# One load queue, 4 MB chunks and a hand-fixed order in an attention decode with a gated mixer

## The chip, the cores and the metric

The kernel runs on one core of one Trainium2 chip. The metric is the device time of one execution in microseconds (us), the median of several executions; lower is better. A profiled execution gives a "span", which is the same execution seen by the hardware profiler and about 2 us shorter than the device time.

## The reference, cut to what matters

One token attends to a cache of 65536 keys: 8 K/V heads, 16 query heads, head size 256. Beside it a small mixer makes a row `b`, and a gate mixes the two.

```python
x = A_x                                           # [1, 1, 448], all inputs bf16
g = sigmoid((x * gate_w).sum(-1))
q = (x @ wq)                                      # 16 heads of 256
s = einsum("bhqd,bhkd->bhqk", q, k) * 256**-0.5   # k_cache [1, 8, 65536, 256]
a = softmax(s) @ v                                # v_cache [1, 8, 65536, 256]
a = a.reshape(1, 1, 4096) @ wo
h = layernorm(x)                                  # the mixer: 448 x 1792 elements of gelu
u = gelu(einsum("bsd,sf->bdf", h, w1) + b1)       # w1 [1, 1792]
b = (einsum("bdf,fs->bds", u, w2) + b2)           # w2 [1792, 1]
out = g * a + (1 - g) * b
```

K and V are 537 MB of the 544 MB that have to be read. So this is first of all a matter of how fast one core can take data in.

## The kernel before

It walks through K and V in chunks of 2048 keys (1 MB of K, 1 MB of V, each a row of 8 KB for each of 128 partitions). K goes through the SyncE queue into 4 buffers, V through the ScalarE queue into 5. Each chunk of K is transposed on TensorE (32 transposes of 128x128 bf16), evicted by VectorE (copied out of PSUM, where matmuls leave their results) in four pieces of 128x1024, multiplied by q to give scores, put through `exp`, transposed in 32x32 blocks by VectorE, and multiplied by V. The order of instructions is chosen by an automatic scheduler; the code gives only the data flow. The mixer's 14 blocks stand in one piece behind the first head.

```python
CH = 2048
NJ = CH // 128
NKN = 4
NKT = 2
NVBUF = 5
# ...
    const = ctx.enter_context(tc.tile_pool(name="const", bufs=1))
# ...
    kn_tiles = [knpool.tile([128, NJ, DH], BF16, name=f"kn{i}") for i in range(NKN)]
    v_tiles = [vpool.tile([128, NJ, DH], BF16, name=f"vt{i}") for i in range(NVBUF)]
# ...
            k_src = A_k_cache[0, g, t0:t0 + CH, :].rearrange("(p j) d -> p j d", j=NJ)
            nc.sync.dma_start(out=kn[:, :, :], in_=k_src)
            v_src = A_v_cache[0, g, t0:t0 + CH, :].rearrange("(p j) d -> p j d", j=NJ)
            nc.scalar.dma_start(out=vt[:, :, :], in_=v_src)

            bank_i = 0
            for c in range(2):
                for j0 in range(0, NJ, 8):
                    tp = tps[bank_i % 2]
                    for jj in range(8):
                        j = j0 + jj
                        nc.tensor.transpose(tp[:, jj * 128:(jj + 1) * 128],
                                            kn[:, j, c * 128:(c + 1) * 128], ident[:, :])
                    nc.vector.tensor_copy(out=kT[:, c, j0:j0 + 8, :],
                                          in_=tp[:, :].rearrange("p (j n) -> p j n", j=8))
                    bank_i += 1
            # ... scores of this chunk: 8 matmuls of 512 columns
            if pending is not None:
                pv_matmuls(pv, *pending)          # P times V of the chunk before
            # ... exp on ScalarE
            nc.vector.transpose(out=pT[:, :], in_=p_sb[:, :])
            pending = (pT, vt, (ck == 0), (ck == n_chunks - 1))
        pv_matmuls(pv, *pending)
        if g == 0:
            mixer_mlp()                           # 14 blocks in one piece
        # ... normalise, turn and multiply by wo: the head's epilogue
```

The softmax here doesn't subtract the row's maximum and nothing guards it: scores larger than these inputs give would overflow.

## Time and profile before

| | before |
|---|---|
| median of 3 runs | 1354.73 us (1353.54 to 1356.97) |
| profiled span | 1353.1 us |
| data moved, rate on the plateau | 546.4 MB, 420 GB/s |
| PE, DVE, ACT busy | 73%, 65%, 15% |
| an 8 KB packet of K or V | 312 ns median |

In profiles PE stands for TensorE, PEld for its weight loads, DVE for VectorE, ACT for ScalarE, POOL for GpSimd and SP for SyncE; a q behind a name, as in SPq, is that engine issuing DMAs. From the page of the kernel before: busy time of each engine, two of the lines that cut the span into 40 equal slices (busy tenths of the DMA engines, and what they moved), then the load queues, the instruction fetch and the data read.

```profile
span 1353.1 us, 33043 instructions
PE 990.1 (73%) x14602; PEld 658.7 (49%) x14602; DVE 876.8 (65%) x1665; ACT 196.7 (15%) x554; POOL 8.2 (1%) x21
...
DMA  9999997899999999999999999999999999999994
GB/s 279 396 418 420 419 420 324 350 420 420 419 420 420 420 419 419 420 419 420 419 415 411 420 420 413 418 418 416 420 414 413 418 419 416 420 401 419 419 420 181
...
q1 hardware_dynamic: 37250, 272.12, 49.2%
q10 hardware_dynamic: 36864, 268.45, 48.3%
...
q8 instruction: 114, 1.87, 0.6%
...
HBM read 544.22 MB, written 0.00 MB: 402 GB/s over the span
```

No compute engine is near its limit. The DMA engines are, in nearly every slice. A slice is 33.8 us long. Where it shows 420 the kernel can only become faster if the stream itself does; where it shows less, something else held the stream up. This gives a ledger. For each slice the lost time is its length times (1 − its rate ÷ the plateau's rate); what remains of the span is the stream. The plateau is read off the slices, and one GB/s more or less there moves about 3 us between the stream and the other terms.

| us | stream at its plateau | lost in slices 0–1 (start) | 2–7 (mixer) | 8–37 (middle) | 38–39 (end) |
|---|---|---|---|---|---|
| before, 420 GB/s | 1300.9 | 13.3 | 13.6 | 6.0 | 19.2 |

The dip in slices 6 and 7 is the mixer. The table by stretches of the kernel before shows it: stretch, its length, busy time (and instructions) of PE, weight load, DVE, ACT and POOL, then the granted PE clock, the DMA share and GB/s. The last two lines are the end, where the data stops.

```profile
220.00:230.00 10.00, 9.66 (x81) 5.38 (x79) 5.90 (x11) 1.80 (x4) 0.00 (x0) 0.67 0.53 209
230.00:240.00 10.00, 10.00 (x71) 4.69 (x73) 7.76 (x18) 2.79 (x6) 0.00 (x0) 0.67 0.73 285
...
1335.00:1340.00 5.00, 3.43 (x59) 2.37 (x57) 3.46 (x8) 0.80 (x4) 0.00 (x0) 1.00 0.20 84
1340.00:1345.00 5.00, 2.88 (x55) 1.40 (x52) 3.08 (x7) 0.69 (x2) 0.00 (x0) 1.00 0.01 3
```

In these 20 us PE is full while the clock is down to 0.67, and the stream is at half to two thirds of its rate: there the mixer, not DMA, bounds the kernel. At the end 15 us of serial work remain after the last data. The PE lines of the timeline (start, duration, what it is, in brackets the idle time before it and what ended it) show its two ends:

```profile
1335.66 0.61 PE L295 MATMUL tps_128<-ident,kn_112 128*128 128x128 bf16 x8 [0.34 <-DVE kT_114 L300]
1337.92 0.56 PE L295 MATMUL tps_127<-ident,kn_113 128*128 128x128 bf16 x7 [0.90 <-DMA kn_113<-in_A_k_cache_dram]
...
1344.46 0.61 PE L260 MATMUL pv_ps_135<-vt_116,pT_124 128*2 128x256 bf16 x16 [1.66 <-DVE pv_sb L336]
```

The second line is the last time that PE waits for data. The first one also gives a cost: eight bf16 transposes in 0.61 us.

### The profile page before, as it was taken

Reading aid. Unit: us, or ns where it says so; the run is one execution under the profiler, and the core shown is the slowest. Engines: PE = TensorE matmul, PEld = TensorE weight load, DVE = VectorE, ACT = ScalarE, POOL = GpSimd, SP = SyncE. Lnnn points to the kernel's source line nnn. Section 1 sums busy time; section 2 is a strip of 40 time slices with the busy share of each in tenths; the row PEclk is TensorE's granted clock in tenths of the full one; section 3 lists DMA queues with packets and bytes.
Section 4 is the critical chain, followed back from the end, with each engine's and each line's share of the span. In section 5 each row is a group of like instructions: output and inputs, shape, how many; then the busy total and the mean of one; then the engine's idle time right before and its main releaser. Section 6 shows DMA issues by size and latency. Waiting matters only on the chain. (4 is left out here: it accounts for less than half of the span.)

```text
span 1353.1 us, 33043 instructions
## 1 busy us (share of the span) xinstructions
PE 990.1 (73%) x14602; PEld 658.7 (49%) x14602; DVE 876.8 (65%) x1665; ACT 196.7 (15%) x554; POOL 8.2 (1%) x21
## 2 busy tenths in 40 slices
PE   2887889867687776776677666767768767777775
PEld 2555555545454454544445444544445444544453
DVE  1567677866666666666666666666666666666665
ACT  0111122111111111111111111111111111111111
POOL 2000000000000000000000000000000000000000
PEclk9989897998999889899998999999999999989988
DMA  9999997899999999999999999999999999999994
GB/s 279 396 418 420 419 420 324 350 420 420 419 420 420 420 419 419 420 419 420 419 415 411 420 420 413 418 418 416 420 414 413 418 419 416 420 401 419 419 420 181
DMA packets 75281, 546.37 MB, mean 404 GB/s; under 512 B 8657, under 2 KB 8674, under 8 KB 9490
## 3 DMA queue, kind: packets, MB, share of 16 engines
q1 hardware_dynamic: 37250, 272.12, 49.2%
q10 hardware_dynamic: 36864, 268.45, 48.3%
q0 software_dynamic: 1024, 3.69, 0.7%
q8 instruction: 114, 1.87, 0.6%
q14 instruction: 29, 0.24, 0.0%
HBM read 544.22 MB, written 0.00 MB: 402 GB/s over the span
## 5 line engine op out<-in xcount | busy, mean ns | idle before, releaser
L300 DVE COPY kT_115<-tps_127 128x1024 bf16<-128x1024 bf16 x256 | 175.1, 684 | 137.2 <-PE tps_127 L295 136.7
L300 DVE COPY kT_114<-tps_127 128x1024 bf16<-128x1024 bf16 x256 | 174.9, 683 | 126.0 <-PE tps_127 L295 125.1
L300 DVE COPY kT_115<-tps_128 128x1024 bf16<-128x1024 bf16 x256 | 173.2, 677 | 85.1 <-PE tps_128 L295 81.9
L300 DVE COPY kT_114<-tps_128 128x1024 bf16<-128x1024 bf16 x256 | 173.5, 678 | 84.5 <-PE tps_128 L295 82.0
L295 PEld LDWEIGHTS <-kn_111 128*128 128x128 bf16 x2048 | 128.9, 103 | 150.2 <-DMA kn_111<-in_A_k_cache_dram 94.3
L295 PEld LDWEIGHTS <-kn_112 128*128 128x128 bf16 x2048 | 128.2, 103 | 140.9 <-DMA kn_112<-in_A_k_cache_dram 80.0
L295 PEld LDWEIGHTS <-kn_113 128*128 128x128 bf16 x2048 | 126.7, 102 | 135.5 <-DMA kn_113<-in_A_k_cache_dram 77.8
L295 PEld LDWEIGHTS <-kn_110 128*128 128x128 bf16 x2048 | 126.4, 102 | 126.6 <-DMA kn_110<-in_A_k_cache_dram 74.0
L319 ACT ACTIVATE p_sb_122<-sc_ps_133 128x512 bf16<-128x512 f32 x128 | 76.4, 597 | 545.1 <-issue 348.6
L319 ACT ACTIVATE p_sb_121<-sc_ps_132 128x512 bf16<-128x512 f32 x128 | 76.4, 597 | 515.3 <-issue 346.8
L295 PE MATMUL tps_127<-ident,kn_111 128*128 128x128 bf16 x1024 | 86.4, 230 | 78.2 <-DMA kn_111<-in_A_k_cache_dram 68.6
L295 PE MATMUL tps_127<-ident,kn_112 128*128 128x128 bf16 x1024 | 88.0, 230 | 65.0 <-DMA kn_112<-in_A_k_cache_dram 50.7
L295 PE MATMUL tps_127<-ident,kn_113 128*128 128x128 bf16 x1024 | 87.1, 230 | 66.2 <-DMA kn_113<-in_A_k_cache_dram 57.9
L295 PE MATMUL tps_127<-ident,kn_110 128*128 128x128 bf16 x1024 | 84.7, 228 | 58.2 <-DMA kn_110<-in_A_k_cache_dram 47.3
L308 PE MATMUL sc_ps_133<-kT_115,qT_sb 128*2 128x512 bf16 x1024 | 117.4, 401 | 0.4 <-DVE kT_115 L300 0.4
L308 PE MATMUL sc_ps_132<-kT_114,qT_sb 128*2 128x512 bf16 x1024 | 112.5, 396 | 0.5 <-DVE kT_114 L300 0.3
L295 PE MATMUL tps_128<-ident,kn_111 128*128 128x128 bf16 x1024 | 88.8, 231 | 15.7 <-DVE kT_115 L300 15.6
L295 PE MATMUL tps_128<-ident,kn_112 128*128 128x128 bf16 x1024 | 87.7, 230 | 15.2 <-DVE kT_114 L300 14.9
L295 PE MATMUL tps_128<-ident,kn_110 128*128 128x128 bf16 x1024 | 85.2, 227 | 16.9 <-DVE kT_114 L300 16.9
L295 PE MATMUL tps_128<-ident,kn_113 128*128 128x128 bf16 x1024 | 85.7, 228 | 14.5 <-DVE kT_115 L300 14.5
L326 DVE STREAM_TRANSPOSE pT_124<-p_sb_122 128x512 bf16<-128x512 bf16 x128 | 90.0, 703 | 0.0
L326 DVE STREAM_TRANSPOSE pT_123<-p_sb_121 128x512 bf16<-128x512 bf16 x128 | 89.9, 702 | 0.0
(101 smaller groups left out, 613.9 us busy)
## 6 DMA issues: line engine op xcount, KB each, us to landing
kn_110<-in_A_k_cache_dram SPq DMA_DIRECT2D x64, 1024.0 KB, 16.3
kn_111<-in_A_k_cache_dram SPq DMA_DIRECT2D x64, 1024.0 KB, 16.5
kn_112<-in_A_k_cache_dram SPq DMA_DIRECT2D x64, 1024.0 KB, 16.5
kn_113<-in_A_k_cache_dram SPq DMA_DIRECT2D x64, 1024.0 KB, 16.5
vt_116<-in_A_v_cache_dram ACTq DMA_DIRECT2D x52, 1024.0 KB, 15.3
vt_117<-in_A_v_cache_dram ACTq DMA_DIRECT2D x51, 1024.0 KB, 15.3
vt_118<-in_A_v_cache_dram ACTq DMA_DIRECT2D x51, 1024.0 KB, 15.2
vt_119<-in_A_v_cache_dram ACTq DMA_DIRECT2D x51, 1024.0 KB, 15.3
```

What stands on the lines that cost most here:

```text
L295: nc.tensor.transpose(tp[:, jj * 128:(jj + 1) * 128], kn[:, j, c * 128:(c + 1) * 128], ident[:, :],)
L300: nc.vector.tensor_copy(out=kT[:, c, j0:j0 + 8, :], in_=tp[:, :].rearrange("p (j n) -> p j n", j=8))
L308: nc.tensor.matmul(ps[32 * a:32 * a + 2, :], lhsT=qT_sb[:, c, 2 * g:2 * g + 2], rhs=rhs, start=(c == 0), stop=(c == 1), tile_position=(0, ...
L319: nc.scalar.activation(out=p_sb[:, :], in_=ps[:, :], func=ACT.Exp, scale=inv_sqrt_dh, accum_out=den[:, 0:1],)
L326: nc.vector.transpose(out=pT[:, :], in_=p_sb[:, :])
```

## The change

It is a rewrite with five intents: load everything through one queue in 4 MB chunks, of which 5 lie in a ring in turn (K, V, K, V, ...); transpose K as 32-bit pairs of bf16, which halves the number of transposes; fix the order of all instructions by hand; spread the mixer over the first 30 steps instead of one block; and shorten the epilogue. A step is still 2048 keys, a quarter of a chunk, and there are 256 of them. The product with V lags four steps behind. The core of the new code:

```diff
+    ctx.enter_context(tc.manual_schedule())
+    ring = [ringp.tile([128, NB * DH], BF16, name=f"ring{i}") for i in range(RING)]   # 5 x 32 KB a partition
+    LAST_V = [2 * SB, SB, SB // 2 + 2, SB // 2 - 2]
+    def load(item):                      # even items are K, odd ones V
+        ...
+        parts = [NB]                     # one DMA of 4 MB, rows of 32 KB
+        if i == total - 1:
+            parts = LAST_V if is_v else LAST_K
+        j = 0
+        for n in parts:
+            nc.sync.dma_start(out=dst[:, j * DH:(j + n) * DH], in_=src[:, j * DH:(j + n) * DH])
+            j += n
-                        nc.tensor.transpose(tp[...], kn[:, j, c * 128:(c + 1) * 128], ident[:, :])   # bf16, x32
+        kn = ring[2 * (n // STEPS) % RING][:].bitcast(FP32).rearrange("p (j k) -> p j k", k=128)
+        for jj in range(8):                                                           # fp32, x16
+            nc.tensor.transpose(tp[:, 128 * jj:128 * jj + 128], kn[:, j0 + jj, :], ident[:])
+        nc.vector.tensor_copy(out=kT[n % 2][...], in_=tp[:].bitcast(BF16))            # 128x2048, x2
+    def mixer_close(b):
+        nc.vector.scalar_tensor_tensor(out=gel[:], in0=t_b[:], scalar=1.0, in1=u_b[:], ...)
+        nc.tensor.matmul(y_ps, lhsT=w2T[:, b:b + 1], rhs=gel[:], start=(b == 0), stop=(b == NF - 1))
+    def mixer(n):
+        b, ph = divmod(n - 2, 2)
+        if ph == 0:
+            if 0 < b <= NF:
+                mixer_close(b - 1)
+            if b == NF:
+                mixer_end()
+            if 0 <= b < NF:
+                mixer_open(b)
+        elif 0 <= b < NF:
+            mixer_mid(b)
+    for n in range(n_steps + LAG):
+        transposes(n, 0)
+        scores(n - 1)
+        transposes(n, 1)
+        p_transpose(n - 1)
+        mixer(n)
+        epilogue(n)
+        p_v(n - LAG)
+        ...                              # load the slot that has just come free
```

(Guards at the first and last steps are cut.) In the mixer, `u` is no longer made by matmuls but by DVE, and its square by ACT, each with one scalar for each partition; only the sum over `w2`, called y, is left to PE.

## The prediction

> **What bounds the kernel now.** DMA. The slice view shows the 16 DMA engines at 90% or more in 36 of 40 slices and 415 to 420 GB/s on the plateau; the table by stretches gives 412 to 420 GB/s for every 100 us from 400 to 1300 us. The core must read 544.2 MB (page, HBM read), which alone is 1296 us at 420 GB/s. PE (73%), DVE (65%), ACT (15%) are below it. About 52 us of the 1353 us span are lost against 420 GB/s: about 11 us in the first 25 us (237 GB/s), about 13 us between 210 and 260 us (the mixer's 14 blocks in one piece hold PE and DVE; 209 to 287 GB/s), about 19 us in the last 23 us (data stops by 1338 us, then the serial epilogue to 1353), the rest in small dips.
>
> **What the change does, per step of 2048 keys (K and V: 2.1 MB, 5.0 us at 420 GB/s; 256 steps).**
> - PE: 32 bf16 transposes (8 in 0.61 us in the timeline, so 2.4 us) become 16 of 32-bit pairs. A 32-bit one has no duration in this trace. The Trainium skill, "TensorE: Matmul & The Clock Gate", Terms, says transpose mode is 4x faster for FP32; no run here shows it. If it holds, I estimate 110 to 170 ns each, 1.8 to 2.7 us. Scores stay about 0.8 us, PV (8 of 512 columns for 16 of 256) about 0.8 us. Sum 3.4 to 4.3 us: below 5.0.
> - DVE: four evictions of 128x1024 at 0.68 us become two of 128x2048, estimate 1.2 us each; the 0.70 us stream transpose stays. 3.6 becomes about 3.1 us. The mixer adds about 1 us per step for 30 steps (0.38 and 0.61 us operations): 4.1 us, still below 5.0, so the mixer dip should vanish.
> - DMA: 512 K/V transfers of 1 MB with 8 KB packets on two queues become about 134 on one queue with 32 KB packets; 20 MB of ring. In the trace's packet records an 8 KB packet takes 312 ns, a 4480 B one 179 ns; the difference implies about 10 to 15 ns fixed per packet. Four times fewer packets then give an estimated 426 to 431 GB/s; the skill, "DMA: Bandwidth & Descriptors", Where 436 GB/s comes from, puts the ceiling at 435. One queue instead of two should cost nothing while several transfers are queued.
> - Instruction fetch (1.87 MB) about halves: 2 us.
> - Epilogue: about 9 us after the last bytes instead of 15; the last V is cut so that little remains.
>
> **On the critical path.** Only the stream, its start and end. Mixer dip -13, start -6, tail -7, rate -20, small dips -5, instruction fetch -2. Sum from below: 544.2 MB at 427 is 1274, plus 3 start, plus 10 for the tail: **1287 us**, range 1270 to 1318. Faster 0.91, same 0.04, slower 0.05.
>
> **What would show it.** K packets of 32 KB near 1.22 us; 425 GB/s or more in all slices but the first and last; no dip at 210 to 260 us; PE waiting for the ring's DMA, and the load queue waiting for nothing that stops the stream; last data within 10 us of the end.
>
> **What would make it wrong.** (1) The only 32 KB packets here, the 112 of wq, took 2.14 us each, 15.3 GB/s per engine against 26.3 for 8 KB packets. I put this on its 112 partitions; if it is the packet size, the stream falls far below 420 and the kernel is much slower. (2) If a 32-bit transpose takes over 230 ns, PE exceeds 5.0 us a step and binds. (3) If packet overhead is hidden, the rate stays 420: about 1310 us.

## The result, and the profile after

| | before | after |
|---|---|---|
| median | 1354.65 us | 1304.43 us (4 runs, 1303.6 to 1305.27) |
| ratio, 95% interval | | 0.9632, 0.9617 to 0.9647 |
| profiled span | 1353.1 us | 1303.5 us |
| instructions | 33043 | 19519 |
| mean granted PE clock | 0.939 | 0.852 |
| a packet of K or V | 8 KB, 312 ns | 32 KB, 1213 ns |

Ratios here and below are the mean time of one kernel's runs over the mean of the other's runs of the same rounds, so they are not quite the ratios of the medians that are quoted. Executions over 1.5% slower than the fastest of the same kernel are left out of the means. Each set of runs had its own runs of the kernel before, with medians between 1352.2 and 1354.65 us.

The same lines of the page, after:

```profile
span 1303.5 us, 19519 instructions
PE 962.2 (74%) x8448; PEld 600.4 (46%) x8448; DVE 810.3 (62%) x897; ACT 194.7 (15%) x543; POOL 22.7 (2%) x94
...
GB/s 358 428 421 377 370 354 383 430 432 429 430 432 431 432 433 433 431 432 431 431 433 429 432 432 430 432 430 434 431 432 432 430 433 432 432 433 431 429 429 251
...
q1 hardware_dynamic: 19602, 540.55, 96.9%
...
q8 instruction: 66, 1.08, 0.3%
...
HBM read 544.34 MB, written 0.00 MB: 418 GB/s over the span
```

The plateau rose to 432 GB/s, the start is better, and the dip of two slices became one of four, less deep and longer. The ledger shows what each part was worth:

| us | stream | start | mixer | middle | end | sum |
|---|---|---|---|---|---|---|
| before, 420 GB/s | 1300.9 | 13.3 | 13.6 | 6.0 | 19.2 | 1353.1 |
| after, 432 GB/s | 1263.1 | 5.9 | 19.4 | 1.2 | 13.9 | 1303.5 |
| difference | −37.8 | −7.4 | +5.8 | −4.8 | −5.3 | −49.6 |

So the mixer, which the prediction had down for a gain of 13 us, costs more than before. The table by stretches of the kernel after, in the dip and at the end:

```profile
160.00:170.00 10.00, 7.24 (x54) 4.56 (x53) 7.04 (x9) 1.84 (x5) 0.00 (x0) 0.80 0.59 224
...
1285.00:1290.00 5.00, 5.00 (x57) 2.95 (x49) 4.64 (x6) 1.38 (x4) 0.00 (x0) 1.00 0.60 256
1290.00:1295.00 5.00, 4.22 (x56) 2.40 (x56) 4.33 (x5) 1.08 (x3) 0.00 (x0) 1.00 0.49 203
1295.00:1300.00 5.00, 3.14 (x36) 1.74 (x29) 2.02 (x6) 0.30 (x2) 0.00 (x0) 1.00 0.02 5
```

In the dip neither PE (7.24 of 10 us) nor DVE (7.04) is full, yet the stream is at half its rate (this is the slowest stretch of the dip; others show up to 452 GB/s). This is the mark of waiting, not of work. The waits of PE say on what (engine and line that waits, what ended it: us in total, times, longest):

```profile
PE misc L276 <- DVE gel L273: 43.1, 14, 3.1
```

Once for each of the 14 mixer blocks PE stands 3.1 us before the matmul of y, which needs `gel` from DVE. The timeline of one pair of steps shows what this does:

```profile
130.31 1.09 PE L316 MATMUL tps_75<-ident,ring_72 128*128 128x128 f32 x8
132.14 1.22 DVE L317 COPY kT_325<-tps_75 128x2048 bf16<-128x2048 bf16 x1
133.27 0.70 DVE L338 STREAM_TRANSPOSE pT_334<-p_328 128x512 bf16<-128x512 bf16 x1
133.90 0.58 DVE L273 SCALAR_TENSOR_TENSOR gel<-t_b,u_b 128x448 bf16<-128x448 f32 x1
134.53 0.53 PE L276 MATMUL misc<-gel,w2T 128*1 128x448 bf16 x1 [3.13 <-DVE gel L273]
...
135.85 1.97 PE L316 MATMUL tps_74<-ident,ring_72 128*128 128x128 f32 x8
137.75 1.04 PE L326 MATMUL sc_76<-kT_325,qT 128*32 128x512 bf16 x8
...
146.74 0.35 PE L276 MATMUL misc<-gel,w2T 128*1 128x448 bf16 x1 [3.12 <-DVE gel L273]
```

On DVE `gel` stands behind the eviction of this step's second half and behind the stream transpose of P, which itself waits for the scores and for ACT. PE takes its instructions in order: the Trainium skill, "TensorE: Matmul & The Clock Gate", Step-by-step: what each phase is for, says of the matmuls that they "stay in program order", and the trace agrees, as the next transposes, whose data is long there, start only after y. What follows runs slowly as well: eight transposes take 1.97 us instead of 1.09, eight score matmuls 1.04 instead of 0.62. The same page, HAM oscillation, says that idle gaps longer than about 3.4 us let the clock of PE fall to half; the clock records of this trace agree in kind, at slightly shorter gaps: in or right after each of the 14 waits, 2.4 to 3.1 us long, a stretch of 3.4 or 6.8 us at half clock begins. From one y to the next are 12.2 us for two steps, where the stream at 432 GB/s would bring two steps' data (4.2 MB) in 9.7. Fourteen such pairs would come to 35 us; 19.4 were lost. That the data waiting in the ring took up the difference is argued, not shown.

The load queue waits in its turn, which is the way the delay reaches the stream. From the waits of the queue of SyncE:

```profile
SPq L96 <- PE pv L348: 1168.1, 64, 31.3
```

It waits nearly always for a product with V to free a slot of the ring. That is harmless while other loads are still queued in flight, and the plateau of 432 GB/s shows it is; it stops the stream only when PE is late. At the end, the last product, its scaling and the store of the result:

```profile
1296.91 0.60 PE L348 MATMUL pv<-ring_71,pT_332 128*4 128x512 bf16 x8
1297.57 0.75 DVE L365 TENSOR_SCALAR pvs<-pv,rden 128x512 f32<-128x512 f32 x1 [0.62 <-PE pv L348]
...
1301.28 0.32 SPq L433 DMA_DIRECT2D out_dram<-res  x1
```

The last packets of V move at 1296 us, about 7 us before the end rather than 15. But the 10 us before that run at half rate or little more, which is why the loss at the end is still 13.9 us. The landing records of the last load show why: all loads had been issued by 1276.1 us, but of the 16 DMA engines the first finished its share of the last load at 1284.9 us and the last one at 1296.6. The engines had drifted apart, and the early ones had nothing left to move. As an estimate, half of these 11.7 us and the 7 us after them make up 12.9 of the 13.9.

The trace also keeps a record of every packet. Its medians in ns, which the rest needs:

```
            K and V                     wq                    instruction fetch
before      8 KB:   312 (both queues)   112 of 32 KB: 2142    114 of 16 KB: 1073
after       32 KB: 1213                 24 KB: 941            66 of 16 KB: 937
            8 KB (the last K, part of the last V): 309
```

### The profile page after: what moved, and what is told of

The parts are those of the page before. It is cut to its first block, busy times and chain, and to the rows that moved or that the text cites. A ratio compares the mean times of both kernels' runs of the same rounds, so it can differ in the third digit from the quotient of the medians.

```text
span 1303.5 us, 19519 instructions
## 1 busy us (share of the span) xinstructions
PE 962.2 (74%) x8448; PEld 600.4 (46%) x8448; DVE 810.3 (62%) x897; ACT 194.7 (15%) x543; POOL 22.7 (2%) x94
## 4 chain that ended last, share of the span: by engine, by line
DMA 54%; PE 38%; DVE 7%; issue 1%; ACT 0%; ACTq 0%
PE tps_74 L316 13%; PE tps_75 L316 12%; DMA ring_71<-in_A_k_cache_dram 12%; DMA ring_73<-in_A_k_cache_dram 12%; DMA ring_69<-in_A_k_cache_dram 11%; DMA ring_70<-in_A_k_cache_dram 10%; DMA ring_72<-in_A_k_cache_dram 9%; PE pv L348 6%; PE sc_77 L326 3%; PE sc_76 L326 3%; DVE kT_325 L317 2%; DVE kT_326 L317 1%; DMA xa<-in_A_x_dram 1%; DVE t_b L269 1%; DVE gel L273 1%
## 5 line engine op out<-in xcount | busy, mean ns | idle before, releaser
L317 DVE COPY kT_325<-tps_74 128x2048 bf16<-128x2048 bf16 x128 | 154.8, 1209 | 302.2 <-PE tps_74 L316 302.2
L317 DVE COPY kT_325<-tps_75 128x2048 bf16<-128x2048 bf16 x128 | 156.6, 1224 | 85.6 <-PE tps_75 L316 85.0
L317 DVE COPY kT_326<-tps_74 128x2048 bf16<-128x2048 bf16 x128 | 153.2, 1197 | 43.8 <-PE tps_74 L316 42.8
L317 DVE COPY kT_326<-tps_75 128x2048 bf16<-128x2048 bf16 x128 | 156.8, 1225 | 36.3 <-PE tps_75 L316 36.2
L316 PE MATMUL tps_74<-ident,ring_71 128*128 128x128 f32 x416 | 69.8, 322 | 66.3 <-DMA ring_71<-in_A_k_cache_dram 66.3
L316 PE MATMUL tps_74<-ident,ring_69 128*128 128x128 f32 x416 | 67.8, 316 | 58.5 <-DMA ring_69<-in_A_k_cache_dram 58.5
L316 PE MATMUL tps_74<-ident,ring_73 128*128 128x128 f32 x416 | 69.2, 320 | 53.3 <-DMA ring_73<-in_A_k_cache_dram 53.3
L326 PE MATMUL sc_77<-kT_326,qT 128*32 128x512 bf16 x1024 | 101.6, 481 | 1.2 <-DVE kT_326 L317 1.2
L316 PE MATMUL tps_74<-ident,ring_70 128*128 128x128 f32 x416 | 67.0, 313 | 48.0 <-DMA ring_70<-in_A_k_cache_dram 48.0
L316 PE MATMUL tps_74<-ident,ring_72 128*128 128x128 f32 x384 | 63.6, 319 | 49.0 <-DMA ring_72<-in_A_k_cache_dram 49.0
L316 PEld LDWEIGHTS tps_74<-ident,ring_71 128*128 128x128 f32 x416 | 55.5, 165 | 92.1 <-issue 92.1
L316 PEld LDWEIGHTS tps_74<-ident,ring_69 128*128 128x128 f32 x416 | 54.0, 161 | 81.4 <-issue 72.3
L316 PEld LDWEIGHTS tps_74<-ident,ring_73 128*128 128x128 f32 x416 | 54.8, 163 | 78.5 <-issue 77.6
L316 PEld LDWEIGHTS tps_74<-ident,ring_70 128*128 128x128 f32 x416 | 53.1, 160 | 72.6 <-issue 72.2
L316 PEld LDWEIGHTS tps_74<-ident,ring_72 128*128 128x128 f32 x384 | 50.5, 164 | 72.5 <-issue 70.4
L326 PE MATMUL sc_76<-kT_325,qT 128*32 128x512 bf16 x1024 | 83.2, 402 | 0.2
L316 PE MATMUL tps_75<-ident,ring_71 128*128 128x128 f32 x416 | 65.1, 306 | 0.0
L316 PE MATMUL tps_75<-ident,ring_73 128*128 128x128 f32 x416 | 64.7, 306 | 0.0
L316 PEld LDWEIGHTS tps_75<-ident,ring_73 128*128 128x128 f32 x416 | 51.7, 157 | 28.0 <-issue 28.0
L316 PEld LDWEIGHTS tps_75<-ident,ring_71 128*128 128x128 f32 x416 | 51.6, 157 | 27.9 <-issue 27.9
```

The source lines that it names most:

```text
L316: nc.tensor.transpose(tp[:, 128 * jj:128 * jj + 128], kn[:, j0 + jj, :], ident[:])
L317: nc.vector.tensor_copy(out=kT[n % 2][:, 8 * DH * half:8 * DH * (half + 1)], in_=tp[:].bitcast(BF16))
L326: nc.tensor.matmul(sc[n % 2][32 * a:32 * a + 32, :], lhsT=qT[:, c, g].rearrange("p r x -> p (r x)"), rhs=kv[:, :, 32 * a:32 * a + 32, c], ...
```

## The experiments

The theory to begin with: (A) the stream gained by larger packets, one queue is neutral, and the mixer dip is PE waiting in order for `gel`. Its rivals: (B) the gain in rate came from having one queue, or from the other order of instructions; (C) the dip is DVE or PE having too much work. All twelve kernels gave the correct result.

### e1_y_late: only the matmul of y moves, one step later

```diff
     def mixer_close(b):
         nc.vector.scalar_tensor_tensor(out=gel[:], ...)
+    def mixer_y(b):
         nc.tensor.matmul(y_ps, lhsT=w2T[:, b:b + 1], rhs=gel[:], ...)
@@ mixer(n)
             if 0 < b <= NF:
                 mixer_close(b - 1)
-            if b == NF:
-                mixer_end()
             if 0 <= b < NF:
                 mixer_open(b)
-        elif 0 <= b < NF:
-            mixer_mid(b)
+        else:
+            if 0 < b <= NF:
+                mixer_y(b - 1)
+            if b == NF:
+                mixer_end()
+            if 0 <= b < NF:
+                mixer_mid(b)
```

> Edit: the mixer's one PE matmul per block (y) is issued one step later than its input gel, so PE no longer stands in line for VectorE. Theory A (the dip of 370 to 413 GB/s between 100 and 230 us is PE standing 3.1 us per block behind gel, then working at the lower granted clock; 43 us of waiting for 14 blocks): the pitch of two mixer steps falls from 12.0 us to about 9.7 us or less, the stream stays near 430 GB/s in that stretch, time about 1288 us (1283 to 1294). Rival B (the mixer's 2.1 us of VectorE work per two steps is what exceeds the budget, wherever the matmul stands): dip stays, 1300 to 1305 us.

Measured: 1286.71 us, ratio to before 0.9519 (0.9503 to 0.9534); against the 1304.43 us of the changed kernel that is 17.7 us less. Of the page and of the timeline of this kernel:

```profile
GB/s 367 425 434 429 434 429 432 431 435 428 435 428 435 429 434 429 431 431 433 431 433 428 432 434 431 432 431 431 433 431 434 428 433 434 431 431 427 427 430 250
```

```profile
152.01 0.35 PE L278 MATMUL misc<-gel,w2T 128*1 128x448 bf16 x1
...
153.08 1.09 PE L321 MATMUL tps<-ident,ring 128*128 128x128 f32 x8 [0.28 <-DVE kT L322]
...
159.59 0.35 PE L278 MATMUL misc<-gel,w2T 128*1 128x448 bf16 x1
```

The dip is gone (0.2 us lost instead of 19.4), y starts without any wait, the transposes are back at 1.09 us, and two steps take 7.6 us in this stretch (PE has data in hand here; it then waits for the stream, as it should). The amount of work on every engine is the same as in the changed kernel, one engine's queue has one instruction in another place (the mixer's two closing operations on DVE move with the last of them). The clock still falls to half in this stretch, after waits of 3.0 to 5.1 us for K, and does no harm there. So rival C falls, and this is also the best version.

### e2_8k_packets: the changed kernel with 1 MB loads

```diff
-        parts = [NB]
+        parts = [SB] * STEPS
```

> Edit: every 4 MB load is issued as four 1 MB loads on the same queue, into the same ring, so its packets are 8 KB instead of 32 KB. Theory A (the packet size makes the stream faster): packets of 309 ns (26.5 GB/s an engine) for 1213 ns (27.0), plateau 424 GB/s for 432, about 20 us longer than the changed kernel: 1320 to 1330 us. Rival B (it is the single queue, or the deeper prefetch, that made 420 into 432): plateau stays at 430 or more, 1300 to 1308 us.

Measured: 1303.61 us, ratio 0.9642; the same as the changed kernel. The slices of the page tell another story than the time:

```profile
GB/s 350 427 427 426 425 427 401 425 427 426 426 425 425 426 427 427 424 425 427 426 428 424 426 426 426 427 425 426 426 427 427 424 426 427 426 426 426 427 426 254
```

The plateau is 426 GB/s instead of 432, with packets of 309 ns (four of them 1236 ns, against 1213 for one of 32 KB), and that costs 17.6 us of stream, as e8 will show alone. But the mixer dip shrinks to 1.9 us at the same time, though PE still waits 14 times for `gel`, 43.1 us in all. Two effects of equal size cancelled. Why the dip shrinks is argued, not separated: with quarter chunks PE begins at 19.5 us instead of 26.6, so it is further ahead of the stream when the mixer comes, and pieces of the ring are filled one by one.

### e8_y_late_8k: both edits together

The edits of e1 and e2.

> Edit on e1_y_late: 1 MB loads with 8 KB packets, as in e2. Theory A (packet size is worth 432 against 426 GB/s; in e2 that was hidden, because with 1 MB loads PE starts on the first quarter of a chunk and had the slack to ride over the mixer): 537 MB at 426 for 432 is 17 us, 1300 to 1305 us, no better than e2 without the late matmul. Rival B (packet size is worth nothing in time): 1285 to 1290 us.

Measured: 1303.28 us, ratio 0.9633. Of the page:

```profile
GB/s 352 425 427 425 426 426 425 426 426 426 426 425 426 425 427 427 425 425 427 426 426 424 427 426 427 425 425 427 425 426 427 425 425 426 426 426 426 427 426 242
```

Against e1 (no dip in either) this is the size of load and packet by itself: 426 for 432 GB/s, stream 1280.8 against 1263.2 us, and 16.6 us in the medians. The Trainium skill, "DMA: Bandwidth & Descriptors", Rules for kernel authors, gives 128 partitions and at least 1 MiB for a load as the rule for maximum bandwidth. Both kernels keep it, and still 4 MB loads with 32 KB rows gain 1.4%. As e11 and the packet records show, the row does it: 4 × 309 − 1213 = 23 ns saved over three packets fewer, an estimate of 8 ns for each packet. The last V of the changed kernel, which comes in packets of 16, 8, 5 and 3 KB, agrees: their medians of 611, 309, 196 and 121 ns lie on one line with the 1213 ns, 8 ns and 0.0368 ns a byte.

### e11_y_late_8k_contiguous: the same rows from one contiguous piece of memory

In e8, a 1 MB load takes every 128th part of 4 MB in a stride of 32 KB. Here each load is 1 MB in one piece.

```diff
-        src = src.rearrange("(p j) d -> p (j d)", j=NB)
+        rows.rearrange("(s p j) d -> s p (j d)", s=4, j=16)   # load s reads its own 1 MB
```

> Edit on e8_y_late_8k (1303.3 us): each 1 MB load takes 2048 consecutive keys, 1 MB in one piece of HBM as in the kernel before, instead of every partition's quarter of a 4 MB chunk (8 KB pieces 32 KB apart). Theory A (it is one stream instead of two that makes 309 of 312 ns): packets stay 309 ns, plateau 426, 1301 to 1306 us. Rival B (it is the address pattern): 312 ns, plateau 420 to 422, 1313 to 1322 us.

Measured: 1303.45 us, ratio 0.9623, packets 309 ns. Of these two patterns of addresses in memory neither is faster.

### e12_before_aligned: the kernel before, with its buffers 64 bytes further

A plain comparison leaves a gap: the 8 KB packets take 309 ns in e8 and 312 in before, which is 420 against 426 GB/s. By the addresses in the built programs, the K and V buffers of the kernel before start at SBUF offsets of 192 beyond a multiple of 256 (the first K buffer at 25280, the first V buffer at 74432); the ring starts at 26880, a multiple of 256. One unused tile moves them.

```diff
     b2_row = const.tile([1, 1], FP32)
+    pad = const.tile([128, 16], FP32)      # never used; K then starts at 25344, V at 74496
```

The order of the instructions on every engine stays as it was.

> Edit: one unused tile of 64 bytes a partition ahead of the K and V buffers in the kernel before; the order of instructions on every engine is unchanged. It moves the buffers from SBUF offsets that are 192 modulo 256 to offsets that are 0 modulo 256, as the ring of the changed kernel has. Neither queue count (e10) nor the HBM address pattern (e11) explained why an 8 KB packet takes 312 ns before and 309 ns in the changed kernel. Theory A (the packet's destination has to start on a 256-byte boundary[...]): packets 309 ns, plateau 425 to 426 GB/s, 1334 to 1345 us, ratio 0.986 to 0.993. Rival B (something else in the kernel before slows its packets): 312 ns, 420 GB/s, ratio 0.998 to 1.002.

Measured: 1336.05 us, ratio 0.9877 (0.9855 to 0.99), whose interval lies clear of 1. Of the page:

```profile
GB/s 279 405 423 425 425 426 320 366 425 426 425 425 426 425 425 425 425 425 426 425 426 418 423 425 425 420 422 420 425 425 419 424 424 423 426 409 423 425 425 180
```

The median packet of K and V fell from 312 to 309 ns on both queues, the stream from 1300.9 to 1282.4 us (at 426 GB/s), and all other terms of the ledger stayed (13.2, 13.4, 5.9, 19.3 us). So 18.5 us of the change's 37.8 in the stream have nothing to do with chunks, queues or order. They come from where the buffers happen to lie. Two limits of this: the pad also moves the other buffers that are allocated behind it (`kT`, P, wq) by the same 64 bytes, so that K's and V's own offset is at work is the plainest reading, but not separated. And the offset shows only while the stream is full: in the kernel before itself the median is 309 ns from 220 to 240 us, where the mixer holds the stream at 209 to 285 GB/s, and it is 309 ns in e4 below, whose buffers lie at the same offsets and whose stream runs at about 306 GB/s. Why is open.

### e7_before_wq_8k: is a 32 KB packet slow by itself?

The prediction's first worry: the 112 packets of wq in the kernel before. The load is cut into four with 8 KB rows.

```diff
-    nc.sync.dma_start(out=wqT[:], in_=A_wq.rearrange("(p kc) n -> p kc n", kc=KCX))
+    for kc in range(KCX):
+        nc.sync.dma_start(out=wqT[:, kc, :], in_=A_wq.rearrange("(p kc) n -> p kc n", kc=KCX)[:, kc, :])
```

> Edit: the kernel before, its wq load of 112 rows of 32 KB issued as four loads of 112 rows of 8 KB. Its packets took 2142 ns (15.3 GB/s an engine). Theory A (the 112 partitions make it slow): 8 KB packets of wq take 450 to 550 ns, again about 15 GB/s. Rival B (32 KB packets there were slow by their size): about 310 ns. The whole time may move a little with the scheduler's order and is not the point.

Measured, one look: 1356.1 us. The 448 packets of wq have a median of 474 ns (the middle half 446 to 500), about 17 GB/s for an engine, as slow as the 32 KB packets (15.3) and not as the 8 KB packets of K (26). Packet size is not the cause, as the 1213 ns of the ring's packets say as well. V's first loads on the other queue are not it either: in e4 and e10 below, V follows on the same queue, and the packets of wq still take 1992 and 2051 ns. Whether it is the 112 partitions or the place in SBUF (96 beyond a multiple of 256) stays open.

### e4_before_one_queue: one queue in the kernel before

```diff
-            nc.scalar.dma_start(out=vt[:, :, :], in_=v_src)
+            nc.sync.dma_start(out=vt[:, :, :], in_=v_src)
```

> Edit: the kernel before, with its V loads issued from SyncE like its K loads; everything else unchanged (1 MB loads, 8 KB packets). Theory A (one queue is worth about 3 of 312 ns a packet): packets 309 ns, plateau 422 to 424 GB/s, 1342 to 1350 us, ratio to before 0.991 to 0.997. Rival B (the queue count matters for nothing): ratio 0.998 to 1.002. Rival C (one queue costs, because a V load can stand behind a K load that waits for its buffer): over 1358 us.

Measured: 1806.93 us, ratio 1.3352. This run does not say what it was made for. The scheduler answered the edit with another order: it put each product with V directly behind the scores of its own chunk. The waits of PE and a line of its timeline:

```profile
PE pv_ps L260 <- DVE pT L326: 388.8, 239, 1.9
```

```profile
711.37 1.02 PE L260 MATMUL pv_ps<-vt,pT 128*2 128x256 bf16 x16 [1.66 <-DVE pT L326]
```

For 239 of 256 chunks PE waits for the whole chain from scores through ACT and DVE, 1.66 us; a step then takes about 7 us. The plateau is about 306 GB/s with a packet median of 309 ns, not longer than elsewhere: the packets are not slower, the stream is starved.

### e9_before_as_written and e10_before_as_written_one_queue: the order by hand

To compare queues at one order, the scheduler is turned off in the kernel before, and its instructions stay as the code has them.

```diff
+    ctx.enter_context(tc.manual_schedule())
```

> Edit: the kernel before with two queues as it was, but its instructions in the order in which the program writes them, not the scheduler's. e4_before_one_queue had this very order on PE (32 transposes, 8 scores, 16 PV of the chunk before), so two things had changed there. Theory A (the order cost e4 its 450 us: scores, exponent, stream transpose and PV of one chunk stand one after the other): 1720 to 1830 us. Rival B (it was the single queue, where a load that waits for its buffer holds up the next): 1350 to 1450 us.

e10 has the same line and V on the queue of SyncE as in e4.

> Edit: e9_before_as_written (1514 us) with V issued from SyncE too, so the queue is the only change, which it was not in e4 (there the scheduler had also put the PV of a chunk directly behind the scores of the same chunk). Theory A (two big streams at once are what makes an 8 KB packet take 312 ns instead of 309): packets 309 ns, best slices 424 to 426 GB/s for 420, 1490 to 1508 us. Rival B (queue count costs nothing; the 312 ns have another source): packets 312 ns, 1510 to 1520 us. Rival C (a load waiting for its buffer holds up the load behind it): over 1530 us, with less than 420 GB/s away from the group ends.

Measured: e9 1514.22 us (1.1196), e10 1444.32 us (1.0664). The expectation that e9 would have the bad order of e4 was wrong: as written, the product with V is that of the chunk before, and the plateau is 420. Of the pages of e9 and of e10:

```profile
GB/s 284 402 419 420 417 148 0 0 247 420 419 411 329 382 417 419 415 315 420 419 416 354 363 413 420 415 315 420 419 420 377 348 420 420 421 313 417 421 413 264
```

```profile
GB/s 294 403 420 420 419 349 0 0 103 411 418 421 420 419 419 419 420 421 420 420 419 420 400 420 420 419 413 419 419 420 418 409 420 419 419 395 420 420 419 229
```

Three things follow. The packets take 312 ns with one queue and with two, and the plateau is 420 in both, so rival B falls: the number of queues does not set the rate. The Trainium skill, "DMA: Bandwidth & Descriptors", Rules for kernel authors, says that spreading loads over several issuing engines does not help bandwidth, and the trace agrees. Second, without the scheduler the mixer's block stops the stream almost wholly for two slices; the scheduler of the kernel before was worth 160 us, most of it by spreading the mixer and the head ends. A hand-fixed order needs the mixer spread by hand, and the change did both. Third, one queue was even better than two here: the dips at the ends of heads (slices 12, 17, 21 and so on in e9) are gone in e10. Why is argued only: with K and V in one line, the loads keep the order in which they are used, and V's loads no longer stand in ScalarE's instruction stream between its exponents. The waits fit: in e9 PE waits 217 times for data of V, 193.3 us in all, and in e10 that wait is gone (149 waits for K, 126.7 us, stand there instead).

### e3_v_on_act and e6_two_queues_8k: two queues in the changed kernel

e3 sends V through the queue of ScalarE; e6 does that with the 1 MB loads of e2 and moves the small loads of x to the queue of GpSimd.

```diff
-            nc.sync.dma_start(out=dst[...], in_=src[...])
+            eng = nc.scalar if is_v else nc.sync
+            eng.dma_start(out=dst[...], in_=src[...])
```

> Edit: the V chunks are issued from ScalarE's queue, K stays on SyncE's: two queues with 32 KB packets. Theory A (packet size sets the rate, two queues cost at most 3 ns a packet, as 312 against 309 ns for 8 KB packets): packets near 1216 ns, plateau 430 to 432 GB/s, 1302 to 1312 us. Rival B (one queue is what gains): plateau near 420 GB/s, 1325 us or more.

> Edit on e2_8k_packets: V is issued from ScalarE's queue (and the small x loads from GpSimd's, so that they don't stand behind V). Compared with e2 at 1303.6 us. Theory A (two big streams at once cost each engine some 1% whatever the packet, 312 for 309 ns): packets 312 ns, plateau 420 to 422 GB/s, 1314 to 1325 us. Rival B (the 421 GB/s of e3_v_on_act came from 4 MB K chunks landing late beside V, so PE released the ring late): packets 309 ns, plateau 425 to 426, 1300 to 1308 us.

Measured: e3 1356.66 us (1.0036), e6 1331.88 us (0.984). So two queues take all of the change's gain away in e3, and over half in e6. Of the page of e3, and of e6:

```profile
GB/s 359 371 230 387 343 378 335 433 415 421 411 425 421 431 419 419 420 417 410 427 421 426 428 431 422 413 424 425 424 418 428 393 432 416 429 426 419 429 426 171
```

```profile
GB/s 349 421 427 329 369 338 368 424 426 426 426 426 425 427 426 426 426 425 426 427 426 426 425 426 426 426 424 427 426 426 426 425 419 426 426 427 419 426 427 171
```

In e6 the packets take 309 ns on both queues and the plateau is 426, just as with one queue; the loss is the dip of the mixer (23.5 us) and the end (19.9 us). In e3 the start is spoilt too (the loads of x stand behind V's chunks in the queue of ScalarE, and PE first waits 52 us for the gate's product of x), and the plateau itself is ragged, 421 on average. With two queues a 4 MB chunk of V is fetched beside the chunk of K that PE needs first, so that K comes later (the first one lands at 46.8 us, in the changed kernel at 26.5); how much of e3's loss this makes is not shown. 5% of V's packets take 1491 ns or more in e3, and this I cannot fully explain. In e6 it is not K that comes late, since PE waits only 7.4 us for its data. The waits of e6 show another path, with ScalarE's own work behind V's issues:

```profile
ACT p L333 <- DMA ring<-in_A_k_cache_dram: 258.8, 29, 12.2
ACT p L333 <- DMA ring<-in_A_v_cache_dram: 247.2, 26, 11.4
DVE pT L339 <- ACT p L333: 320.9, 62, 8.0
PE tps L317 <- DVE kT L318: 235.6, 47, 7.5
```

V's loads are issued from ScalarE's instruction stream. An issue that has to wait there for earlier loads holds up the exponent behind it, up to 12.2 us long, then the stream transpose of P on DVE, the eviction behind that, and PE. In the changed kernel ACT has no such wait. That this is what deepens the dip is read from the waits, not tested by itself. What both suggest is that one queue, on an engine that has no other work, is right for this ring, and not for its rate. V on a second queue of an engine without such work was not tried.

### e5_y_late_bf16_transposes: bf16 transposes in the best version

```diff
-    ident = const.tile([128, 128], FP32)
+    ident = const.tile([128, 128], BF16)
@@ transposes
-        kn = ring[...][:].bitcast(FP32).rearrange("p (j k) -> p j k", k=128)
+        kn = ring[...][:].rearrange("p (j k) -> p j k", k=128)
-        tp = tps[half]
+        tp = tps[half][:].bitcast(BF16)
-        for jj in range(8):
+        for jj in range(16):
```

(The views of `kT` and `wq` change with it, since the pairs are no longer interleaved.)

> Edit on e1_y_late: K is transposed as 32 bf16 blocks per step (54 ns each when warm, 2.4 us) instead of 16 blocks of 32-bit pairs (136 ns each, 2.2 us). Theory A (the pairs save PE almost nothing, and PE is not what binds; but some 8000 more PE instructions mean some 30 more 16 KB instruction fetches[...], so the engines drift further apart and the end gets longer): 1287 to 1293 us, plateau 431. Rival B (the pairs are needed to keep PE under the stream's 4.85 us a step): over 1300 us, dips in the plateau.

Measured: 1292.62 us, ratio 0.9553 (0.9534 to 0.9572), 5.9 us slower than e1 by the medians and, since the two ran in different sets, 4.6 us by the ratios. Of its page and its timeline:

```profile
span 1289.0 us, 27643 instructions
...
q8 instruction: 98, 1.61, 0.5%
```

```profile
608.25 1.07 PE L321 MATMUL tps<-ident,ring 128*128 128x128 bf16 x16
```

Sixteen bf16 transposes take 1.07 us, eight of pairs 1.09. So the 32-bit pairs save PE no time at all: half as many, each twice as long. What they save is 8126 instructions, and with them 32 instruction fetches of 16 KB. The Trainium skill, "Runtime: NRT & Kernel Launch", Instruction fetch mechanics, says that a sequencer fetches its instructions in blocks of 16 KiB, 256 instructions, by a DMA queue of its own, and calls the cost mostly hidden; the trace agrees with the size of the blocks. Here it is not hidden in the sum, since the DMA engines are the bottleneck: the middle loses 4.4 us for 1.5, the end 14.7 for 13.7. Fetching 32 more blocks takes 32 × 16 KB ÷ 432 GB/s = 1.2 us by bytes, less than was lost. The rest may be that the 16 DMA engines drift apart: already in e1 the time between the first and the last of them to finish one load grows from 1.9 us at the start to about 11 us at 1000 us, and in e5 it grows faster (7.8 against 5.1 us at 470 us). That the fetches cause the drift is not shown; the trace does not say which engines serve them.

## Why the prediction was right or wrong

The measured time, 1304.43 us, lies in the predicted range, and the direction was right with it. The sum behind the central value of 1287 us had two large errors of opposite sign. Term by term, against the ledger of the span (1287 predicted, 1303.5 measured):

| term | predicted us | measured us | difference |
|---|---|---|---|
| stream | 1274 (427 GB/s) | 1263.1 (432 GB/s) | −10.9 |
| start | 3 | 5.9 | +2.9 |
| mixer dip | 0 | 19.4 | +19.4 |
| middle | 0 | 1.2 | +1.2 |
| end | 10 | 13.9 | +3.9 |

**The step that failed is the mixer's: "4.1 us, still below 5.0, so the mixer dip should vanish."** It compared the summed busy time of DVE with the time of the stream, and the sum was right: neither engine was full in the dip. But a sum says nothing of order. `gel` is made late in a step and the matmul of y stood in PE's queue right behind it, in the same step; PE waited 43.1 us in 14 places, and ran cold after each. e1 moves that one instruction by a step and the dip is gone, 17.7 us. With it the kernel takes 1286.71 us, and this closeness to the predicted 1287 is partly luck, because the other errors cancel.

**The stream's rate: right in its kind, too small in its size, and with half of its cause missed.** "Four times fewer packets" gave 17.6 us (e8 against e1), from 426 to 432. That is about the 20 us that were predicted for the rate, but from a higher base. The other 18.5 us are the placement of the buffers in SBUF (e12), which the prediction did not think of. The remaining 1.7 us of the 37.8 is close to 0.66 MB fewer bytes moved, mostly instructions. The estimate of 10 to 15 ns fixed for a packet was near, 8 ns, but it did not follow from its own numbers: 179 ns for 4480 bytes and 312 ns for 8192 give 18 ns, and these packets differed in more than their size.

The Trainium skill, "DMA: Bandwidth & Descriptors", Where 436 GB/s comes from, was useful in one half: the ceiling of 435 GB/s holds (432 reached). In its other half that section says that about 358 GB/s of the memory side binds for loads from HBM; this is not what one core alone sees here, and the measurement decides. (The same page, under Measured, keeps 358 GB/s for two cores that stream at once and has 425 for one.)

**One queue costs nothing:** right, and shown at equal order by e9 and e10. For the ring a second queue on ScalarE costs time (e3, e6), which the prediction did not say; in e6 the waits put it down to V's issues, which hold up ScalarE.

**PE and DVE below the stream:** right. A step on a warm clock takes 3.13 us of PE in the changed kernel (from 1280.57 to 1283.70 us in its timeline), where 3.4 to 4.3 had been estimated. A transpose of pairs takes about 0.14 us, in the range of 110 to 170 ns; but there is no gain in PE time over bf16 (e5). The skill's "4× faster for FP32" (in the Terms of "TensorE: Matmul & The Clock Gate") was used only to bound this, and no run here compares with a transpose without that mode. DVE takes 2 × 1.22 + 0.70 = 3.14 us a step, as predicted.

**Start and end:** "plus 3 start, plus 10 for the tail" were 5.9 and 13.9. The time after the last data was predicted well (9, measured about 7 us), but the data before it does not come at full rate up to the last byte, as the DMA engines have drifted apart by then.

**The worries:** packets of 32 KB are not slow (1213 ns, and e7), a transpose is far below 230 ns, and the overhead of packets is not hidden. None of the three came true; what did was not in the list.

## What to carry to other kernels

Adding up the busy time of an engine shows whether there is room, not whether an in-order queue will stand: for each instruction ask which engine's newest result it needs, and put it one step behind that result, as here with one matmul that was worth 17.7 us. In a kernel that is bound by loads, look at the packet records first and at where the buffers start in SBUF: a pad of 64 bytes, from 192 beyond a multiple of 256 onto a multiple, was worth about 17 us here, as much as rows four times as long. And where two changes leave the time the same, as in e2, read the slices before saying that nothing happened.

## What the Trainium skill lacked or had wrong

- "SBUF — State Buffer", Operand start alignment, speaks of what is allowed and says that it timed nothing. The cost for a load: with K and V buffers 192 bytes beyond a multiple of 256, an 8 KB packet takes 312 ns and the stream 420 GB/s; at a multiple of 256, 309 ns and 426 GB/s (e12, 1336.05 against 1353.44 us). "DMA: Bandwidth & Descriptors", How a descriptor splits into AXI transactions, tells of 256-byte boundaries where data is read; here it is the place of the destination. Only these two offsets were compared, and the cost shows only with the stream at its plateau (e4: the same offset, about 306 GB/s, 309 ns).
- "DMA: Bandwidth & Descriptors", Where 436 GB/s comes from: the HBM side at about 358 GB/s does not bind one core that loads alone; 432 GB/s over most of 1300 us were measured. The passage does not say that its figure is for two cores at once, as the same page does under Measured.
- "DMA: Bandwidth & Descriptors", Rules for kernel authors: at least 1 MiB for a load is not yet the maximum, also when many loads are in flight (for larger single loads the page's own table under Measured says so). Rows of 32 KB in 4 MB loads gave 432 GB/s, rows of 8 KB in 1 MB loads 426 (e1, e8), whether contiguous or strided (e11).
- "Runtime: NRT & Kernel Launch", Instruction fetch mechanics: the fetch is called mostly hidden, and no cost to a data stream is given. 8126 instructions more, 32 blocks, went with 4.6 to 5.9 us in a kernel bound by DMA (e5), more than their bytes account for; the way is not shown.
- "TensorE: Matmul & The Clock Gate": a transpose of 128x128 32-bit pairs takes about 0.14 us in a row of eight, and two bf16 ones that do the same take as long (1.09 and 1.07 us for a whole half step). No page compares the two.
- No page has: the load of wq with 112 partitions ran at 15.3 to 17 GB/s for a DMA engine, whether in packets of 32 or of 8 KB (e7); the 16 DMA engines drift apart over a long stream, from 1.9 to about 11 us over 1000 us (e1), and the last load is then spread over 11.7 us (the changed kernel). "DMA: Bandwidth & Descriptors", Latency and other measured facts, knows only of two engines that are usually slower; the records here do not name the engines. Both are without a shown cause.
